# Top-32 attention and a cosine-gated feed-forward on one core: the 32 largest found by sixteen and sixteen instead of by pairs

## The chip, the cores and the metric

The kernel runs on one core of a Trainium2 chip. The metric is the device time of one execution in microseconds (us), lower is better. Five engines of the core work side by side, each with its own queue of instructions that it takes in order: TensorE (PE), VectorE (DVE), ScalarE (ACT), GpSimd (POOL) and SyncE (SP, which here only issues DMAs). [...]

## The reference

Eight batches of eight heads, 576 queries and 576 keys each, 64 wide, are attended to over the 32 largest scores of each query; the result, 4608 tokens of 512 values, goes through a feed-forward of 2048 hidden values with the gate h * cos(h).

```python
scores = scale * np.matmul(q, k.transpose(0, 1, 3, 2))          # (8, 8, 576, 576)
kth = np.partition(scores, -top_k, axis=-1)[..., -top_k:-top_k + 1]   # top_k = 32
scores = np.where(scores >= kth, scores, -1000000000.0)
attn = np.exp(scores - np.max(scores, axis=-1, keepdims=True))
attn = attn / (np.sum(attn, axis=-1, keepdims=True) + 1e-09)
x = np.matmul(attn, v)       # brought to (4608, 512)
h = x @ w_in                 # 512 -> 2048
out = (h * np.cos(h)) @ w_out
```

All data are 32-bit floats.

## The kernel before

The 4608 tokens are 36 blocks of 128 rows, and a block has four units, each a pair of heads: 144 units. One call of `slot(i, u, w, x, z)` is written out for each unit i, and the order of its statements is the order of each engine's queue; no scheduler reorders it. In a slot, unit u = i is searched for its 32 largest, unit w = i-1 is masked and exponentiated, unit x = i-2 is sent to be transposed, and z, the four units of a block, are multiplied with V in one slot of four. The feed-forward of an earlier block b is spread over the four slots of a block; m = i % 4 chooses which part. "Slot m2" below is a slot with m = 2.

**Scores.** PE makes the 576 scores of both heads into PSUM (L242, tile `sc`, and its last 128 columns in `rim`); ACT copies them to SBUF as `s` (`take_scores`, L253 and L257). Scores of two units are made in each of m0 and m2, into two buffers.

**Search.** DVE finds the eight largest of a row with one instruction (MAX8, L361) and overwrites them with a very small number with another (MATCH_REPLACE8, L366), so that the next MAX8 finds the next eight. A slot first folds its 576 scores to 288: `fold_high` (L267, DVE) keeps the larger of columns c and c + 288 in `rest`, and the smaller goes to `low`: POOL adds the two as integers (`fold_sum`, L283) and subtracts the larger (`fold_low`, L292). For the units 8 to 10 (`BUSY`) DVE does the smaller too (`fold_now`, L275). Of the larger ones 32 are found in four rounds, of the smaller ones 16 in two, each for both heads: 12 MAX8 and 8 MATCH_REPLACE8, all over 288. In the next slot `merge_first` and `merge_second` (L349, L354) find the 32nd of the two sorted lists, and `distances` (L372) the shift for the exponent.

**Weights of the attention.** ACT masks (`mask`, L380), and takes exponentials with their sums (`exponentials`, L389). DVE adds a small constant and takes the reciprocal (`sums`, `reciprocal`, L397 and L402) between the last two MAX8 of the slot, so that the reciprocals are the last that DVE does in a slot. In the next slot POOL splits the 32-bit exponentials into 16-bit halves (`split_scores`, L412) and then the reciprocals (`split_sums`, L418); SP writes them to memory (L446) and fetches them back transposed (L452) into a ring of five units. In m2 the values of a block are made (L480), and DVE multiplies them with the reciprocals into `xT` (L496), ahead of the last MAX8 pair.

**Feed-forward.** For each block PE makes the hidden values in four banks of 512 (`first_bank`, L543) and the output in four runs (`second_run`, L606). Between them, for each bank: ACT reads the bank twice (`take_first`, L557 and L559), POOL takes the cosine's argument in two instructions (`argument`, L572 and L575), ACT the sine of two banks at once (`sine`, L583), and POOL multiplies (`gate`, L592). Loading a table of exponentials or sines is an ACT instruction of its own.

**POOL's queue before**, from the split on: m0: split, argument of bank 0, fold_sum, fold_low, argument of bank 1. m1: split, gate 0, fold_sum, fold_low, gate 1, argument of bank 2. m2: split, argument of bank 3, fold_sum, fold_low, gates 2 and 3. m3: split, fold_sum, fold_low. In the first dozen slots POOL, DVE and ACT also decode the feed-forward's weights, which come as 64-bit words (`decode_first`, `decode_second`, `decode_third`).

## Time and profile before

| what | value |
|---|---|
| median of 3 runs | 1406.32 us (1405.22 to 1406.49) |
| profiled execution: its own time, and its span | 1406.25 us, 1404.1 us |
| busy: PE, DVE, POOL, ACT | 1347.3, 1337.5, 1197.8, 1140.7 us |
| the chain that ended last: DVE, ACT, PE, POOL | 68%, 18%, 8%, 3% |
| MAX8, all 1728 | 720.7 us busy |
| MATCH_REPLACE8, all 1152 | 502.0 us busy |
| first `fold_high`, 15th (unit 14), last (unit 143) | 7.78, 152.07, 1332.99 us |

The span is the time from the first to the last instruction of the profiled execution; its own time has 2.15 us more. The lines of a profile name the engine, the line of the kernel, the operation, the tile written and the tiles read, partitions x elements, and a count. A busy time counts each instruction to its end, while the next may start before that: the distance from start to start (the chain's pieces) says what an instruction costs its engine.

### The profile page before, as it was taken

How to read it: one execution, taken by the hardware profiler on the slowest of the kernel's cores; microseconds unless marked ns; L12 is line 12 of the kernel's file. 1: busy time of each engine (PE TensorE's matmuls, PEld its weight loads, DVE VectorE, ACT ScalarE, POOL GpSimd, SP SyncE). 2: the span in 40 equal slices, each digit the busy share in tenths (PEclk: the TensorE clock that was granted, in tenths of full speed). 3: DMA queues.
4: the chain of work that ended last, by engine and by line, in shares of the span. 5: the costliest groups of instructions: out<-in, count | busy, mean ns of one | idle time of the engine just before them, and what ended most of it. 6: DMA issues, size and time to landing. Idle time of an engine off the chain costs nothing.

```text
span 1404.1 us, 43874 instructions
## 1 busy us (share of the span) xinstructions
PE 1347.3 (96%) x17024; PEld 906.3 (65%) x17024; DVE 1337.5 (95%) x5012; ACT 1140.7 (81%) x2043; POOL 1197.8 (85%) x1008
## 2 busy tenths in 40 slices
PE   5569999999999999999999999999999999999998
PEld 3355666666666666666666666666666666776665
DVE  7998999999999999999999999999999999999941
ACT  6978888888888888888888888888888888888842
POOL 4787999999999999999999999999999999999920
PEclk9789999999999999999999999999999999999999
DMA  9567775768566586767756568666768566555640
GB/s 285 191 195 188 191 191 152 200 177 200 165 167 168 158 195 172 182 166 176 193 165 176 151 171 198 165 176 163 207 169 175 145 165 172 156 155 144 159 121 16
DMA packets 427488, 240.87 MB, mean 172 GB/s; under 512 B 375952, under 2 KB 392592, under 8 KB 427280
## 3 DMA queue, kind: packets, MB, share of 16 engines
q1 hardware_dynamic: 420720, 224.22, 61.2%
q10 hardware_dynamic: 6560, 13.85, 3.0%
q8 instruction: 133, 2.18, 0.7%
q14 instruction: 75, 0.61, 0.1%
HBM read 45.09 MB, written 101.19 MB: 104 GB/s over the span
## 4 chain that ended last, share of the span: by engine, by line
DVE 68%; ACT 18%; PE 8%; POOL 3%; issue 1%; DMA 1%; ACTq 0%; POOLq 0%; DVEq 0%
DVE top L361 32%; DVE rest L366 18%; DVE rest L267 7%; DVE low L366 6%; ACT s L389 4%; ACT s L380 4%; PE o L606 3%; ACT L583 3%; PE mm L543 3%; ACT x L583 2%; ACT s L253 2%; PE rim L480 2%; ACT s L257 2%; DVE xT L496 1%; DMA ring<-rows 1%
## 5 line engine op out<-in xcount | busy, mean ns | idle before, releaser
L543 PEld LDWEIGHTS mm<-xT,w_in 128*64 128x64 f32 x9216 | 509.5, 137 | 68.2 <-issue 30.3
L543 PE MATMUL mm<-xT,w_in 128*64 128x128 f32 x9216 | 523.7, 273 | 2.7 <-ACT x L559 1.7
L606 PE MATMUL o<-w_out,g 128*64 128x512 f32 x2304 | 521.8, 595 | 3.1 <-POOL g L592 3.1
L361 DVE MAX8 top<-rest 128x8 f32<-128x288 f32 x1152 | 478.9, 451 | 0.0
L366 DVE MATCH_REPLACE8 rest<-top,rest 128x288 f32<-128x288 f32 x864 | 376.6, 443 | 0.0
L380 ACT ACTIVATE s<-s,top 128x576 f32<-128x576 f32 x288 | 207.7, 769 | 189.0 <-DVE top L354 130.3
L606 PEld LDWEIGHTS o<-w_out,g 128*64 128x64 f32 x2304 | 160.6, 137 | 257.6 <-issue 253.2
L412 POOL COPY halves<-s 128x2304 uint16<-128x2304 uint16 x140 | 294.6, 2104 | 35.7 <-ACT s L389 22.3
L361 DVE MAX8 top<-low 128x8 f32<-128x288 f32 x576 | 241.8, 449 | 1.5 <-POOL low L292 1.5
L389 ACT ACTIVATE s<-s,nd 128x576 f32<-128x576 f32 x288 | 220.8, 769 | 2.2
L292 POOL TENSOR_TENSOR low<-low,rest 128x576 int32<-128x576 int32 x141 | 199.8, 1417 | 11.0
L283 POOL TENSOR_TENSOR low<-s 128x576 int32<-128x576 int32 x141 | 200.0, 1418 | 6.5 <-ACT s L259 6.5
L592 POOL TENSOR_TENSOR g<-g,x 128x512 f32<-128x512 f32 x136 | 172.5, 1279 | 16.4 <-ACT x L583 16.4
L575 POOL TENSOR_TENSOR x<-g,x 128x512 f32<-128x512 f32 x136 | 174.0, 1279 | 11.4
L242 PE MATMUL sc<-k,q 64*64 64x448 f32 (+1 forms) x1120 | 147.9, 568 | 14.4 <-DMA k<-in_k_dram 7.4
L480 PE MATMUL rim<-ring,v 128*64 128x128 f32 (+1 forms) x2560 | 138.8, 267 | 0.2 <-issue 0.2
L480 PEld LDWEIGHTS rim<-ring,v 128*64 128x64 f32 x2560 | 129.5, 139 | 6.8 <-issue 6.3
L253 ACT COPY s<-sc 128x896 f32<-128x896 f32 (+1 forms) x144 | 128.0, 889 | 3.4 <-PE sc L242 3.4
L366 DVE MATCH_REPLACE8 low<-top,low 128x288 f32<-128x288 f32 x288 | 125.4, 443 | 0.0
L267 DVE TENSOR_TENSOR rest<-sc,s 128x576 f32<-128x576 f32 x144 | 107.7, 748 | 6.8 <-ACT s L259 6.8
L257 ACT COPY s<-rim 64x256 f32<-64x256 f32 (+1 forms) x280 | 102.8, 367 | 6.9 <-PE rim L480 5.2
L242 PEld LDWEIGHTS rim<-k,q 64*64 64x64 f32 (+1 forms) x1120 | 49.0, 139 | 75.6 <-issue 60.1
(55 smaller groups left out, 1210.1 us busy)
## 6 DMA issues: line engine op xcount, KB each, us to landing
rows<-halves SPq DMA_DIRECT2D x140, 640.0 KB, 3.5
out_dram<-ob ACTq DMA_DIRECT2D x36, 256.0 KB, 3.9
q<-in_q_dram SPq DMA_DIRECT2D x31, 288.0 KB, 5.0
st<-in_moe_w_in_dram SPq DMA_DIRECT2D x16, 512.0 KB, 6.9
v<-in_v_dram SPq DMA_DIRECT2D x32, 256.0 KB, 4.4
k<-in_k_dram SPq DMA_DIRECT2D x31, 144.0 KB, 4.5
k<-in_k_dram SPq DMA_DIRECT2D x32, 128.0 KB, 4.4
st<-in_moe_w_out_dram SPq DMA_DIRECT2D x8, 512.0 KB, 5.6
```

What stands on the lines that cost most here:

```text
L242: nc.tensor.matmul(to[r0 : r0 + rows, rim_bank(r0, j) if k0 else place(u["hp"], j), 0 : k1 - k0], st["q"][d, q0 : q0 + rows], st["k"][d, k ...
L267: nc.vector.tensor_tensor(out=u["rest"][:, :, HS:S], in0=sc[:, :, 0:HS], in1=s[:, :, HS:S], op=ALU.max)
L283: nc.gpsimd.tensor_tensor(out=u["low"].bitcast(I32), in0=s[:, :, 0:HS], in1=s[:, :, HS:S], op=ALU.add)
L292: nc.gpsimd.tensor_tensor(out=low, in0=low, in1=u["rest"][:, :, HS:S].bitcast(I32), op=ALU.subtract)
L361: nc.vector.max(to[:, j], src[:, j])
L366: nc.vector.match_replace(rest[:, j], to[:, j], src[:, j], NEG)
L380: nc.scalar.activation(out=s[:, j], in_=s[:, j], func=AF.Prelu, bias=less[:, j], scale=1.0, alpha=FAR)
L389: nc.scalar.activation(out=s[:, j], in_=s[:, j], func=AF.Exp, bias=nd[:, j : j + 1], scale=SCALE, accum_out=den[:, j, 0:1],)
L412: nc.gpsimd.tensor_copy(out=halves[:, :, 0 : 2 * S], in_=s.rearrange("p (k h) -> p h k", h=2))
L480: nc.tensor.matmul(to[d, r], lhsT, rhs, start=(bank, j) not in begun, stop=c == NT - 1 and u in us[-2:] and r0 + rows == P,)
L543: nc.tensor.matmul(mm[r0 : r0 + D, a * P : (a + 1) * P], w_in[f // FC][:, c, (f % FC) * P + r0 : (f % FC) * P + r0 + D], blk["xT"][:, c], ...
L606: nc.tensor.matmul(blk["o"][r0 : r0 + D], g[:, at : at + D], w_out[f], start=f == 0, stop=f == NF - 1)
```

## The change

The 32 largest are found in another way: sixteen of the 288 larger ones, in two rounds over 288; then sixteen of all that is left, in two rounds over 576, the 272 larger ones left (with the sixteen overwritten) and the 288 smaller ones side by side in `rest`. The 16th largest of the larger ones has at most 15 smaller partners above it, so these are the same 32. The last one found is the 32nd: one small DVE instruction (`threshold`) takes the place of the two merges. The smaller ones are therefore read from the third of four rounds on. In slots m1 from unit 9 on, DVE makes them itself (`by_vector`).

The split is written at the end of the slot of the exponentials (unit w) and no longer at the start of the next one; POOL has the same instructions on either side of that border, so what changes is what stands behind the split. POOL's queue is now: m0: fold_sum, fold_low, argument 1, split. m1: gates 0 and 1, split, arguments 2 and 3. m2: fold_sum, fold_low, gates 2 and 3, split. m3: fold_sum, fold_low, split, argument 0. Against the queue before, fold_sum and fold_low of m1 are gone, and argument 2 and gate 1 have changed sides: gate 1 stands ahead of the split, argument 2 behind it.

On ACT the exponentials are moved ahead of `take_first` of bank 1 (m0) and bank 2 (m1), in m2 the sine of banks 2 and 3 ahead of the exponentials, and in m3 `take_first` of bank 0 ahead of the mask. PE's order is the same up to the last few groups; there the values of the last four units are made together. A load of V may no longer be issued with the send of a block's last unit, and one piece of the weights is loaded three slots earlier.

```diff
@@ -258,40 +258,40 @@
         if at:
             nc.scalar.copy(out=s[:, :, 0:at], in_=u["sc"][:, :, 0:at])
 
+    def by_vector(u):
+
+        return u["n"] in BUSY or u["n"] % NP == 1 and u["n"] > NP + 2
+
     def fold_high(u):
 
         s, sc = u["s"], u["sc"]
-        if u["n"] not in BUSY:
+        if not by_vector(u):
             del u["sc"]
-        u["rest"] = work.tile([P, 2, S], F32, tag="rest", name="rest", bufs=1)
+        u["high"] = work.tile([P, 2, HS], F32, tag="high", name="high", bufs=1)
         nc.vector.tensor_tensor(
-            out=u["rest"][:, :, HS:S], in0=sc[:, :, 0:HS], in1=s[:, :, HS:S], op=ALU.max
+            out=u["high"], in0=sc[:, :, 0:HS], in1=s[:, :, HS:S], op=ALU.max
         )
 
     def fold_now(u):
 
         s, sc = u["s"], u.pop("sc")
-        u["low"] = work.tile([P, 2, HS], F32, tag="low", name="low", bufs=1)
         nc.vector.tensor_tensor(
-            out=u["low"], in0=sc[:, :, 0:HS], in1=s[:, :, HS:S], op=ALU.min
+            out=u["rest"][:, :, HS:S], in0=sc[:, :, 0:HS], in1=s[:, :, HS:S], op=ALU.min
         )
 
     def fold_sum(u):
 
         s = u["s"].bitcast(I32)
-        u["low"] = work.tile([P, 2, HS], F32, tag="low", name="low", bufs=1)
         nc.gpsimd.tensor_tensor(
-            out=u["low"].bitcast(I32), in0=s[:, :, 0:HS], in1=s[:, :, HS:S], op=ALU.add
+            out=u["rest"].bitcast(I32)[:, :, HS:S], in0=s[:, :, 0:HS], in1=s[:, :, HS:S], op=ALU.add
         )
 
     def fold_low(u):
 
-        if u["n"] in BUSY:
+        if by_vector(u):
             return
-        low = u["low"].bitcast(I32)
-        nc.gpsimd.tensor_tensor(
-            out=low, in0=low, in1=u["rest"][:, :, HS:S].bitcast(I32), op=ALU.subtract
-        )
+        low = u["rest"].bitcast(I32)[:, :, HS:S]
+        nc.gpsimd.tensor_tensor(out=low, in0=low, in1=u["high"].bitcast(I32), op=ALU.subtract)
 
     dens = []
     for i in range(2):
@@ -301,58 +301,36 @@
 
     tops = []
     for i in range(2):
-        t = consts.tile([P, 2, TOPK + 1, 2], F32, tag=f"top{i}", name=f"top{i}")
-        nc.vector.memset(t[:, :, 0, 1], -NEG)
-        tops.append(t)
-
-
-
-    def topk_first(u, w, ahead=()):
+        tops.append(consts.tile([P, 2, TOPK + 1], F32, tag=f"top{i}", name=f"top{i}"))
+
+    def topk_first(u, w):
 
         u["top"] = tops[u["n"] % len(tops)]
+        u["rest"] = work.tile([P, 2, S], F32, tag="rest", name="rest", bufs=1)
         if w:
-            merge_first(w)
-        for step in ahead:
-            step()
-        if u["n"] not in BUSY:
+            threshold(w)
+        if not by_vector(u):
             fold_sum(u)
         fold_high(u)
-        if w:
-            merge_second(w)
-        if u["n"] in BUSY:
+        if by_vector(u):
             fold_now(u)
-        topk_round(u, 0, [lambda: distances(w), lambda: None] if w else ())
+        search(
+            u["top"][:, :, 1:9], u["high"], u["rest"][:, :, 0:HS], True,
+            [lambda: distances(w), lambda: None] if w else (),
+        )
 
     def topk_round(u, rnd, between=(), ahead=None):
-        top, rest, lasts = u["top"], u["rest"], TOPK // 8 - 1
-        end = TOPK - 1 - 8 * rnd
-        at = top[:, :, end : end - 8 if rnd < lasts else None : -1, 0]
-        search(
-            at, rest[:, :, HS:S] if rnd == 0 else rest[:, :, 0:HS], rest[:, :, 0:HS], rnd < lasts,
-            between if rnd < lasts else (),
-        )
-        if rnd < lasts:
-            return
-        del u["rest"]
-        low = u.pop("low")
-        for k in range(TOPK // 16):
-            more = k < TOPK // 16 - 1
-            if ahead and not more:
-                ahead()
-            search(top[:, :, 1 + 8 * k : 9 + 8 * k, 1], low, low, more, () if more else between)
-
-
-
-    def merge_first(u):
-        n = TOPK // 2 + 1
-        u["lesser"] = u["top"].rearrange("p j r i -> p j (r i)")[:, :, 2 * n : 3 * n]
+        if ahead:
+            ahead()
+        some = u["rest"][:, :, 0 : HS if rnd == 1 else S]
+        search(u["top"][:, :, 1 + 8 * rnd : 9 + 8 * rnd], some, some, rnd < TOPK // 8 - 1, between)
+        if rnd == TOPK // 8 - 1:
+            del u["rest"], u["high"]
+
+    def threshold(u):
+        u["less"] = u["top"][:, :, 0:1]
         nc.vector.tensor_reduce(
-            out=u["lesser"], in_=u["top"][:, :, 0:n], axis=mybir.AxisListType.X, op=ALU.min
-        )
-
-    def merge_second(u):
-        nc.vector.tensor_reduce(
-            out=u["top"][:, :, TOPK - 1, 1], in_=u.pop("lesser"), axis=mybir.AxisListType.X,
+            out=u["top"][:, :, 0], in_=u["top"][:, :, TOPK : TOPK + 1], axis=mybir.AxisListType.X,
             op=ALU.max, negate=True,
         )
 
@@ -366,11 +344,9 @@
                 nc.vector.match_replace(rest[:, j], to[:, j], src[:, j], NEG)
 
     def distances(u):
-        top = u.pop("top").rearrange("p j r i -> p j (r i)")
-        u["less"] = top[:, :, 2 * TOPK - 1 : 2 * TOPK]
         u["nd"] = small.tile([P, 2], F32, tag="nd", name="nd")
         nc.vector.tensor_reduce(
-            out=u["nd"], in_=top[:, :, 2 * TOPK - 2 : 2 * TOPK], axis=mybir.AxisListType.X, op=ALU.add
+            out=u["nd"], in_=u.pop("top")[:, :, 0:2], axis=mybir.AxisListType.X, op=ALU.add
         )
 
     def mask(u):
@@ -404,16 +380,13 @@
     def both(u):
         return [lambda: sums(u), lambda: reciprocal(u)] if u else ()
 
-    def split_scores(u):
+    def split(u):
 
 
         s = u.pop("s").rearrange("p j k -> p (j k)").bitcast(U16)
         halves = u["halves"] = work.tile([P, 2, 2 * S + P], U16, tag="halves", name="halves", bufs=1)
         nc.gpsimd.tensor_copy(out=halves[:, :, 0 : 2 * S], in_=s.rearrange("p (k h) -> p h k", h=2))
 
-    def split_sums(u):
-
-        halves = u["halves"]
         rden = u.pop("rden").bitcast(U16).rearrange("p (j h) -> p h j", h=2)
         nc.gpsimd.tensor_copy(
             out=halves[:, :, 2 * S :].rearrange("p h (j d) -> p h j d", j=2),
@@ -638,7 +611,7 @@
     at_slot, at_once = {}, {}
 
     def load_at(i, *what):
-        while i in at_slot or (what[0] is load_v and i % NP == 0):
+        while i in at_slot or (what[0] is load_v and i % NP == 3):
             i += 1
         at_slot[i] = what
 
@@ -662,72 +635,70 @@
     for i, u in enumerate(units):
         u["n"] = i
 
-    def send(x, between=()):
-
-        split_scores(x)
-        split_sums(x)
-        for step in between:
-            step()
+    def send(x):
+
+        split(x)
         write_halves(x)
-        for load, b, hp in at_send.pop(x["n"] + 2, ()):
+        for load, b, hp in at_send.pop(x["n"] + 1, ()):
             load(b, hp)
         transposes(x)
 
     def slot(i, u, w, x, z):
         m, b = i % NP, (i - NP - 2) // NP
-        n = (3, 4, 3, 4, 4, 3, 2, 2, 0, 2, 2, 0)[i] if i < 3 * NP else 0
+        n = (3, 4, 3, 4, 4, 3, 2, 3, 0, 2, 1)[i] if i < 2 * NP + 3 else 0 if m == 0 else 2
         if i < NP:
             for load, bb, hp in at_once[i]:
                 load(bb, hp)
         load_weights(n, nc.sync if i < NP + 2 else nc.scalar)
-        if x:
-            (turn if i < NP + 2 else send)(x)
-        if m == 1:
-            gate(b, 0)
-        elif m == 0:
-            argument(b, 0)
-        topk_first(u, w, [lambda: argument(b - 1, 3)] if m == 2 else ())
+        if x and i < NP + 2:
+            turn(x)
+        topk_first(u, w)
         fold_low(u)
-        topk_round(u, 1)
-        topk_round(u, 2)
         if i > 1:
             decode_second(NP)
             decode_third()
+        topk_round(u, 1)
+        topk_round(u, 2)
 
         for o in scored.get(i, []):
             scores(o)
         if z:
             values(z)
-        if m == 1:
+        if m == 0:
+            second_run(b - 1, 3)
+        elif m == 1:
+            gate(b, 0)
             gate(b, 1)
-        elif m == 0:
-            second_run(b - 1, 3)
+            first_bank(b, 3)
         elif m == 2:
             second_run(b - 1, 1)
-        elif m == 3:
+        else:
             second_run(b - 1, 2)
+            take_first(b, 0)
+            first_bank(b, 1)
 
         if w:
             mask(w)
+        if m == 2:
+            sine(b - 1, 1)
+            gate(b - 1, 2)
+            gate(b - 1, 3)
+        if w:
+            exponentials(w)
         if m == 0:
             take_first(b, 1)
             argument(b, 1)
             first_bank(b, 2)
         elif m == 1:
             take_first(b, 2)
-            argument(b, 2)
-            first_bank(b, 3)
             second_run(b, 0)
-        if w:
-            exponentials(w)
-        if m == 3:
-            take_first(b, 0)
-        elif m == 2:
-            sine(b - 1, 1)
-            gate(b - 1, 2)
-            gate(b - 1, 3)
         if i + 1 < NU:
             take_scores(units[i + 1])
+        if m == 0:
+            sine(b, 0)
+            take_second(b - 1)
+        elif m == 1:
+            take_first(b, 3)
 
         def ahead():
             if z:
@@ -740,28 +711,25 @@
         if i == 0:
             decode_second(NP)
             decode_third()
-        if m == 2:
+        if w and i > NP:
+            send(w)
+        if m == 1:
+            argument(b, 2)
+            argument(b, 3)
+        elif m == 2:
             first_bank(b, 0)
         elif m == 3:
-            first_bank(b, 1)
-        elif m == 0:
-            sine(b, 0)
-            take_second(b - 1)
-        elif m == 1:
-            take_first(b, 3)
+            argument(b, 0)
         decode_first(NP)
...
```

More of the change, by code (lines that the diff above doesn't have):

```diff
@@ L757, in drain @@
         ff["end"] = True
-        w, x, last_two = units[NU - 1], units[NU - 2], units[NU - 2 :]
-        send(x)
-        argument(b, 0)
+        w, last = units[NU - 1], units[NU - NP :]
+        threshold(w)
+        distances(w)
         second_run(b - 1, 3)
-        merge_first(w)
-        merge_second(w)
-        distances(w)
         mask(w)
@@ L776, in drain @@
         take_second(b - 1)
+        first_bank(b, 3)
         take_first(b, 2)
-        first_bank(b, 3)
         argument(b, 2)
@@ L782, in drain @@
         argument(b, 3)
-        second_run(b, 1)
         sine(b, 1)
@@ L786, in drain @@
         gate(b, 3)
-        values(units[NU - 4 : NU - 2])
-        take_values(units[NU - 4 : NU - 2])
-        second_run(b, 2)
-        values(last_two)
-        take_values(last_two)
-        second_run(b, 3)
+        values(last)
+        take_values(last)
+        second_run(b, 1)
         b += 1
         first_bank(b, 0)
-        take_second(b - 1)
         take_first(b, 0)
         argument(b, 0)
+        second_run(b - 1, 2)
+        first_bank(b, 1)
+        second_run(b - 1, 3)
+        take_second(b - 1)
         for k in range(1, BANKS):
-            first_bank(b, k)
             take_first(b, k)
             argument(b, k)
+            if k < BANKS - 1:
+                first_bank(b, k + 1)
             if k % 2 == 1:
```

## The prediction

> **What bounds the kernel now.** First the page's chain that ended last, by engine:

> ```profile
> DVE 68%; ACT 18%; PE 8%; POOL 3%; issue 1%; DMA 1%; ACTq 0%; POOLq 0%; DVEq 0%
> ```

> DVE carries it. The timeline of DVE shows how evenly (start, duration, what); these are `fold_high` of units 14, 78, 79, 82 and 143:

> ```profile
> 152.07 0.75 DVE L267 TENSOR_TENSOR rest<-sc,s 128x576 f32<-128x576 f32 x1
> ...
> 737.94 0.75 DVE L267 TENSOR_TENSOR rest<-sc,s 128x576 f32<-128x576 f32 x1
> 747.79 0.75 DVE L267 TENSOR_TENSOR rest<-sc,s 128x576 f32<-128x576 f32 x1
> ...
> 774.58 0.75 DVE L267 TENSOR_TENSOR rest<-sc,s 128x576 f32<-128x576 f32 x1
> ...
> 1332.99 0.75 DVE L267 TENSOR_TENSOR rest<-sc,s 128x576 f32<-128x576 f32 x1
> ```

> From unit 14 to 143 there are 129 slots in 1180.92 us, 32.25 periods of four slots at 36.62 us. Slot m2 (unit 78) takes 9.85 us, since it has the product with the reciprocals; the other three take (774.58 - 747.79) / 3 = 8.93. How close PE is behind shows on its timeline; these are the same two banks, one block apart, in the tightest period:

> ```profile
> 252.08 7.16 PE L543 MATMUL mm<-xT,w_in 128*64 128x128 f32 x128
> ...
> 288.22 7.16 PE L543 MATMUL mm<-xT,w_in 128*64 128x128 f32 x128
> ```

> 36.14 us: in that period PE's groups follow each other without a gap. So PE allows at most 0.48 us a period less than now, whatever DVE gains.

> What DVE's slot consists of is read from the chain in order of time (start, length up to the next piece, what), slot m0 of unit 80:

> ```profile
> 756.60 0.20 DVE top L349
> 756.80 0.66 DVE rest L267
> 757.46 0.10 DVE top L354
> 757.56 0.40 DVE top L361
> ...
> 759.23 0.72 DVE top L361 x2
> 759.95 0.86 DVE rest L366 x2
> 760.81 0.72 DVE top L361 x2
> ```

> A MAX8 over 288 costs DVE 0.36 us and a MATCH_REPLACE8 0.43. The third round begins 4.21 us after the slot. And POOL's queue at the same border of slots, from its timeline:

> ```profile
> 756.66 0.40 POOL L418 COPY halves<-rden 128x256 uint16<-128x256 uint16 x1 [1.30 <-DVE rden L402]
> 757.04 0.62 POOL L572 TENSOR_SCALAR x<-x 128x512 f32<-128x512 int32 x1
> 757.74 1.28 POOL L575 TENSOR_TENSOR x<-g,x 128x512 f32<-128x512 f32 x1
> 758.97 1.41 POOL L283 TENSOR_TENSOR low<-s 128x576 int32<-128x576 int32 x1
> 760.47 1.42 POOL L292 TENSOR_TENSOR low<-low,rest 128x576 int32<-128x576 int32 x1
> ```

> POOL waited here for the reciprocals, which DVE makes last in its slot, and went on 0.06 us after DVE's slot began. Copying them costs 0.38 us, an argument 1.93 (757.04 to 758.97), `fold_sum` 1.50, `fold_low` 1.42. The smaller halves are there at 761.89, 5.29 us into DVE's slot. The kernel before reads them behind four rounds and so doesn't wait: from the third round's 4.21 two more rounds of 0.72 and 0.86, less the last overwriting, put that at 4.21 + 1.58 + 0.72 = 6.51.

> **The search.** It removes 12 MAX8 and 8 MATCH_REPLACE8 over 288: 12 x 0.36 + 8 x 0.43 = 7.76 us. It adds four of each over 288 (3.16) and four MAX8 and two MATCH_REPLACE8 over 576, which the trace doesn't have. How DVE's time grows with length, from the groups by line (count | busy us, mean ns):

> ```profile
> L361 DVE MAX8 top<-rest 128x8 f32<-128x288 f32 x1152 | 478.9, 451 | 0.0
> L366 DVE MATCH_REPLACE8 rest<-top,rest 128x288 f32<-128x288 f32 x864 | 376.6, 443 | 0.0
> ...
> L504 DVE TENSOR_TENSOR xT<-rim,ring 128x128 f32<-128x128 f32 x28 | 6.8, 284 | 5.2 <-ACT s L257 4.7
> ...
> L592 DVE TENSOR_TENSOR g<-g,x 128x512 f32<-128x512 f32 x8 | 5.2, 688 | 4.9 <-ACT x L583 4.9
> ```

> Between 128 and 512 columns (688 - 284) / 384 = 1.05 ns a column; the search instructions at 288 lie on the same line (284 + 160 x 1.05 = 452 against 451 and 443). So 288 columns more are 0.30 us: a long MAX8 0.66, a long MATCH_REPLACE8 0.73, in all 4 x 0.66 + 2 x 0.73 = 4.10. Ends: the slope to the 576 of `fold_high` (0.75 - 0.688 over 64 columns, 0.94) gives 0.63 and 0.70; twice the short one gives 0.72 and 0.86. I take 0.30, the slope with the longest base. The search then costs 7.26 in place of 7.76: 0.50 us less a slot (0.68 to 0.00 at the ends).

> [...]

> **The merges.** L349 and L354 go, 0.20 and 0.10 us on the chain, and one reduction of two columns comes. MAX8 must still wait for the whole 0.75 of `fold_high`, against 0.66 + 0.10 now, so between 0 and 0.25 are left; I take 0.10, since the 0.20 alone lies outside that wait and half of it goes to the new reduction. A slot without a wait: 8.93 - 0.50 - 0.10 = 8.33.

> **Slots m1.** DVE makes the smaller halves: one more instruction of `fold_high`'s form, 0.66 on the chain (ends 0.66 and 0.75). POOL loses 1.50 + 1.42 there; POOL isn't what DVE waits for in m1, so that gives nothing directly.

> **The moved split and the earlier reading.** This decides. The third round now reads the smaller halves, 4.21 - 0.10 = 4.11 us into the slot. POOL can't begin them until the reciprocals are copied, since the split stands ahead in its queue, and that is 0.06 + 0.38 us into DVE's slot at the earliest. From there:
> - m3: split, then the two folds: 0.44 + 1.50 + 1.42 = 3.36. No wait.
> - m0: argument 0 stands between: 5.29. DVE waits 5.29 + 0.02 - 4.11 = 1.20 (0.02 from POOL's end to DVE's start is an estimate; ends 0 and 0.1).
> - m2: arguments 2 and 3 both stand between: 5.29 + 1.93 = 7.22. DVE waits 3.13.
> - m1: no fold on POOL.

> The wait isn't made good later, because the reciprocals that release POOL for the next slot come at the end of the delayed one. A period is 36.62 - 4 x 0.60 + 0.66 + 1.20 + 3.13 = 39.21 us, 2.59 more. PE's 36.14 lies under it. In 32.25 periods: +83.5 us.

> **ACT.** Its sequence in a slot m2, from the chain:

> ```profile
> 738.88 1.44 ACT s L380 x2
> 740.32 0.10 ACT nd L383
> 740.45 1.63 ACT s L389 x4
> 742.09 1.28 ACT L583
> 743.38 1.15 ACT x L583
> 744.53 0.79 ACT s L253
> ```

> In m2 the sine now stands ahead of the exponentials and waits for argument 3, which POOL ends 0.44 + 3.86 = 4.30 into the slot. Sine 1.15, the exponentials' table 1.28, exponentials 1.63 and the scores' copy (0.79, and its last columns, estimated at the same again) end at 9.9, in a slot that now lasts 8.33 + 0.92 + 3.13 = 12.4: hidden, by 2.5 us. In m3 reading bank 0 stands ahead of the mask. That bank needs `xT`, which DVE makes in m2 behind the third round, at 7.24 + 4.10 - 1.32 = 10.0 to 10.8; PE's bank takes half of 7.16, to 14.4, two us into m3. Two readings of 512 columns (estimated from 0.79 for 896: 1.1), mask, exponentials and copy (1.44 + 0.10 + 1.63 + 1.58) end at 20.2, and the next slot's fold comes at 12.4 + 8.33 = 20.7. Hidden by 0.5 us only; this is the second rival.

> **SP and DMA.** The send is the same 140 writes and transposed reads. Reading V moves from the border into m0 to other sends; the order on SP changes, no bytes. In steady slots I cost it nothing: the slots got longer, and the ring is written a slot and more ahead of its use. Cover gone, it would delay the values, which m2 has some 3 us of room for.

> **Start and end.** Up to unit 14 the slots are longer than 8.93 (152.07 us for 14) because of decoding. There the search's 0.60 us can be gained in slots 0 to 4 and 6 to 9, 9 x 0.60 = 5.4 at most, and none if ACT or POOL hold it; I take 4. Slots 8 to 10 have no fold on POOL in either kernel. At the end PE works off the last groups in both, with the same groups: 0, ends -3 and +3.

> **The sum.** Span 1404.1 + 83.5 - 4 = 1483.6; the profiled execution's time is 2.15 us more than its span, and 0.07 under the median: **1486 us**. One us per period more or less is 32 us.

> **The rivals.**
> 1. *PE becomes the bound, faster.* If the folds were ready within 4.11 us in each slot, DVE's period would be 34.9, and PE's 36.14 would decide: 1406.3 - 32.25 x 0.48 - 4 = 1387 us. For it POOL may have no more than 0.75 us between the reciprocals' copy and `fold_sum`; one argument has 1.93. Not slower at all needs both waits together under 1.7 us. The rows of POOL speak against it: it takes its queue in order, and the arguments stand in it. What speaks for it: POOL loses 2.92 us a period, and is idle before the reciprocals as quoted.
> 2. *A second wait on top.* The copy of the scores behind bank 0 in m3 arrives late. Its margin is 0.5 us with two estimates in it; each us beyond costs 32. At 1 us late: 1518 us.
> 3. *Only the wait in m2 holds*, because argument 0 finds its place while POOL waits: 1486 - 32.25 x 1.20 = 1447 us. Against it: argument 0 is behind the reciprocals, as in the quoted rows.
> 4. *Long searches don't overlap.* If each started only at the end of the one before, the four long MAX8 cost 0.09 more (0.451 - 0.36) and the two long MATCH_REPLACE8 about as much: 0.54 a slot, 2.2 a period, 1557 us. The 0.36 us from start to start in the quoted rows speaks against it. [...]

> **Chances.** Forecast 0.66 (its own range 1465 to 1505: waits and merges at their ends), rival 2 0.15, rival 3 0.08, rival 1 0.07, rival 4 0.04. The range reaches from rival 3 to a little above rival 2 and to two thirds of the upper end of the search (+64): 1440 to 1535. A change of 0.2% is about what a measurement here can tell from none. Slower 0.93, same 0.01, faster 0.06.

> **What would show it.** Right: DVE idle before the MAX8 of the third round, released by POOL's subtraction, some 3.1 us in m2 and 1.2 in m0, about 140 us in all, none in m3; PE with gaps of 3 us a period; MAX8 over 576 at 750 ns. Wrong: no DVE idle there, or the folds found ahead of the arguments on POOL; long searches far from 750 ns; DVE waiting for ACT's copy of the scores at the start of m0.

## The result, and the profile after

The changed kernel takes 1570.24 us (median of 4 runs, 1569.53 to 1571.31), the kernel before 1406.40 beside it: a ratio of 1.1168, 95% interval 1.1148 to 1.1187. Slower was right; 1486 us was 84 too low, and the time lies above the range, which ended at 1535.

The page after: its span, the chain that ended last by engine, the granted clock in 40 slices, and two of its costliest groups.

```profile
span 1568.7 us, 42579 instructions
...
PEclk6679999999999989999999989999999998999999
...
PE 76%; issue 7%; DVE 6%; POOL 4%; DMA 3%; ACT 2%; SPq 1%; DVEq 0%; POOLq 0%; ACTq 0%
...
L339 DVE MAX8 top<-rest 128x8 f32<-128x576 f32 (+1 forms) x864 | 534.0, 649 | 161.4 <-POOL rest L294 161.3
...
L271 DVE TENSOR_TENSOR high<-sc,s 128x576 f32<-128x576 f32 x144 | 108.7, 755 | 27.0 <-ACT s L257 20.8
```

DVE carried 68% of the chain before. Now PE carries 76%, although its instructions are the same. DVE idles 161 us for POOL's subtraction, against some 140 forecast, and 21 us for ACT's copy of the scores, which the prediction had named as the sign that it would be wrong.

DVE's timeline gives the slots, by the start of the folds of units 74 to 78 (m2, m3, m0, m1, next m2), the waits before the third round in m2 and m0, and the long MAX8:

```profile
779.61 0.76 DVE L271 TENSOR_TENSOR high<-sc,s 128x576 f32<-128x576 f32 x1
...
786.80 1.42 DVE L339 MAX8 top<-rest 128x8 f32<-128x576 f32 x2 [3.10 <-POOL rest L294]
...
790.97 0.76 DVE L339 MAX8 top<-rest 128x8 f32<-128x576 f32 x1
791.63 0.15 DVE L378 RECIPROCAL rden<-den 128x2 f32<-128x2 f32 x1
...
791.83 0.75 DVE L271 TENSOR_TENSOR high<-sc,s 128x576 f32<-128x576 f32 x1
...
801.02 0.76 DVE L271 TENSOR_TENSOR high<-sc,s 128x576 f32<-128x576 f32 x1 [0.41 <-ACT s L257]
...
806.91 1.42 DVE L339 MAX8 top<-rest 128x8 f32<-128x576 f32 x2 [1.79 <-POOL rest L294]
...
811.29 0.76 DVE L271 TENSOR_TENSOR high<-sc,s 128x576 f32<-128x576 f32 x1
...
820.20 0.76 DVE L271 TENSOR_TENSOR high<-sc,s 128x576 f32<-128x576 f32 x1
```

m2 takes 12.22 us, m3 9.19, m0 10.27, m1 8.91: 40.59 in all, where 39.21 was forecast. The wait in m2 is 3.10 (forecast 3.13) and m1 is 8.91 (8.99). What is over lies in m3, 0.83 us longer than the wait-free slot of 8.36 that five periods show, and in m0, where the wait is 1.79 in place of 1.20.

That makes 32.25 x (40.59 - 36.62) = 128 us; the folds of units 14 and 143 are 1343.04 us apart, 162.1 more than before. The other 34 us lie in four places. A batch is four and a half blocks, so that at every other change of batch a block holds rows of two batches: the units 16, 52, 88 and 124 on (below: the changes of batch; the three changes between two blocks cost nothing). There PE's timeline shows waits for keys, here in slots 52 and 54:

```profile
555.09 2.55 PE L242 MATMUL sc<-k,q 64*64 64x448 f32 x3 [3.57 <-DMA k<-in_k_dram]
...
577.41 1.22 PE L242 MATMUL sc<-k,q 64*64 64x448 f32 x3 [2.23 <-DMA k<-in_k_dram]
```

Slots 52 to 54 last 11.1, 12.3 and 17.1 us, against 10.3, 8.9 and 12.2 in other periods: 9.1 us more. By the same count the other three places (slots 16, 88 and 124 on) take 7.8, 7.6 and 9.0 more, 33.5 in all. The start is 1.7 us later, where the forecast had it 4 earlier, and what follows the last fold is 0.8 longer.

So two things were missing: some 45 us (128 less the forecast 83) spread over the slots m3 and m0, and some 34 at the changes of batch. The second has a plain suspect in the code. In both kernels a load of queries or keys is hung on the send of a numbered slot. `send` in slot i popped those of slot i at the start of that slot, and now pops them at its end.

The first shows on PE. Here is the same output run of 16 instructions in three periods that follow each other:

```profile
737.65 3.65 PE L579 MATMUL o<-w_out,g 128*64 128x512 f32 x16 [2.61 <-issue]
...
776.87 5.28 PE L579 MATMUL o<-w_out,g 128*64 128x512 f32 x16 [2.75 <-issue]
...
817.46 5.35 PE L579 MATMUL o<-w_out,g 128*64 128x512 f32 x16 [2.61 <-issue]
```

PE stands 2.6 us before this run in each, and the run of the same work then takes 3.65 us or 5.3. After 3.65 the next comes 39.22 us later, which is the forecast period (39.21); after 5.28 it is 40.59. The clock is the difference. In two stretches of 6 us that hold these runs (busy us and instructions of PE, PEld, DVE, ACT, POOL; granted clock; DMA share; GB/s):

```profile
736.00:742.00 6.00, 4.35 (x24) 1.62 (x28) 5.96 (x17) 5.64 (x12) 3.62 (x4) 1.00 0.56 136
...
816.00:822.00 6.00, 4.54 (x14) 1.79 (x16) 5.97 (x17) 5.63 (x13) 3.80 (x4) 0.72 0.64 149
```

Clock 1.00 and 0.72, and within the run of 5.35 us it is 0.50, as the last section shows. The gap is new, and the prediction gave it only as a sign ("PE with gaps of 3 us a period") without a price. On ACT's timeline of that slot m1 the reading of bank 2 (L530, L532) now stands behind the exponentials:

```profile
815.46 0.76 ACT L365 ACTIVATE s<-s,nd 128x576 f32<-128x576 f32 x1
...
816.22 0.57 ACT L530 ACTIVATE g<-mm 128x512 f32<-128x512 f32 x1
816.69 0.67 ACT L532 ACTIVATE x<-mm,quarter 128x512 int32<-128x512 f32 x1
```

It ends at 817.36, and PE goes on at 817.46. What a halved clock does to the bank that the next slot needs is on PE's timeline too, bank 0 in the period after the run of 3.65 and after that of 5.28:

```profile
750.75 3.77 PE L516 MATMUL mm<-xT,w_in 128*64 128x128 f32 x64
...
791.59 3.66 PE L516 MATMUL mm<-xT,w_in 128*64 128x128 f32 x64
```

It ends 14.1 us after the fold of its slot m2 in the first (754.52 - 740.39) and 15.6 in the second (795.25 - 779.61). ACT begins to read it at 795.30, and mask, exponentials and the scores' copy of m3 stand behind that. POOL's next split waits for the exponentials, and argument 0 and the folds of m0 stand behind the split:

```profile
795.30 0.60 ACT L530 ACTIVATE g<-mm 128x512 f32<-128x512 f32 x1 [5.83 <-PE mm L516]
...
799.62 2.10 POOL L388 COPY halves<-s 128x2304 uint16<-128x2304 uint16 x1 [4.51 <-ACT s L365]
```

The five slots m3 of 8.36 us between units 14 and 143 are just those that follow a run of 3.65 us behind such a gap (the sixth such run stands ahead of the last slot).

### The profile page after: what moved, and what is told of

The parts are those of the page before. It is cut to its first block, busy times and chain, and to the rows that moved or that the text cites. A ratio compares the mean times of both kernels' runs of the same rounds, so it can differ in the third digit from the quotient of the medians.

```text
span 1568.7 us, 42579 instructions
## 1 busy us (share of the span) xinstructions
PE 1411.1 (90%) x17024; PEld 927.9 (59%) x17024; DVE 1283.0 (82%) x3746; ACT 1145.1 (73%) x2043; POOL 1113.2 (71%) x944
## 4 chain that ended last, share of the span: by engine, by line
PE 76%; issue 7%; DVE 6%; POOL 4%; DMA 3%; ACT 2%; SPq 1%; DVEq 0%; POOLq 0%; ACTq 0%
PE o L579 31%; PE mm L516 27%; PE rim L453 9%; PE sc L242 7%; DVE top L339 3%; PE rim L242 2%; DMA k<-in_k_dram 2%; DVE rest L344 2%; POOL halves L388 1%; DMA rows<-halves 1%; ACT s L365 1%; ACT s L356 1%; DVE high L271 0%; POOL x L548 0%; POOL rest L294 0%
## 5 line engine op out<-in xcount | busy, mean ns | idle before, releaser
L339 DVE MAX8 top<-rest 128x8 f32<-128x576 f32 (+1 forms) x864 | 534.0, 649 | 161.4 <-POOL rest L294 161.3
L579 PE MATMUL o<-w_out,g 128*64 128x512 f32 x2304 | 570.3, 641 | 85.1 <-issue 85.1
L344 DVE MATCH_REPLACE8 rest<-top,rest 128x288 f32<-128x288 f32 (+1 forms) x576 | 337.0, 593 | 0.0
L530 ACT ACTIVATE g<-mm 128x512 f32<-128x512 f32 x144 | 85.2, 592 | 214.1 <-PE mm L516 211.6
L356 ACT ACTIVATE s<-s,top 128x576 f32<-128x576 f32 x288 | 207.6, 770 | 39.7 <-DVE top L332 37.2
L242 PE MATMUL sc<-k,q 64*64 64x448 f32 (+1 forms) x1120 | 166.8, 572 | 36.1 <-DMA k<-in_k_dram 25.5
L548 POOL TENSOR_TENSOR x<-g,x 128x512 f32<-128x512 f32 x137 | 175.0, 1277 | 11.4
L285 POOL TENSOR_TENSOR rest<-s 128x576 int32<-128x576 int32 x108 | 153.9, 1425 | 8.6 <-ACT s L259 5.9
L294 POOL TENSOR_TENSOR rest<-rest,high 128x576 int32<-128x576 int32 x108 | 153.4, 1420 | 8.5
L257 ACT COPY s<-rim 64x256 f32<-64x256 f32 (+1 forms) x280 | 102.9, 367 | 40.9 <-PE rim L453 19.9
L271 DVE TENSOR_TENSOR high<-sc,s 128x576 f32<-128x576 f32 x144 | 108.7, 755 | 27.0 <-ACT s L257 20.8
L253 ACT COPY s<-sc 128x896 f32<-128x896 f32 (+1 forms) x144 | 128.0, 889 | 2.9 <-PE sc L242 2.9
L339 DVE MAX8 top<-high 128x8 f32<-128x288 f32 x288 | 127.1, 455 | 3.7
L556 ACT ACTIVATE x<-x,halfpi 128x1024 f32<-128x1024 f32 x72 | 82.7, 1149 | 64.1 <-POOL x L548 61.4
```

Source lines behind the costliest of these rows:

```text
L242: nc.tensor.matmul(to[r0 : r0 + rows, rim_bank(r0, j) if k0 else place(u["hp"], j), 0 : k1 - k0], st["q"][d, q0 : q0 + rows], st["k"][d, k ...
L285: nc.gpsimd.tensor_tensor(out=u["rest"].bitcast(I32)[:, :, HS:S], in0=s[:, :, 0:HS], in1=s[:, :, HS:S], op=ALU.add)
L339: nc.vector.max(to[:, j], src[:, j])
L344: nc.vector.match_replace(rest[:, j], to[:, j], src[:, j], NEG)
L356: nc.scalar.activation(out=s[:, j], in_=s[:, j], func=AF.Prelu, bias=less[:, j], scale=1.0, alpha=FAR)
L548: nc.gpsimd.tensor_tensor(out=x, in0=g, in1=x, op=ALU.subtract)
```

## The experiments

First theory: late loads cost some 35 us, and the gap, through the clock and bank 0, some 40 to 45. Rival: the waits in m0 and m3 come from the queues of POOL and ACT alone, whatever PE does. A time that is given below without a ratio is that of one execution.

**Loads back to the earlier send (e1_loads).** Changed kernel, with:

```diff
-        while i in at_slot or (what[0] is load_v and i % NP == 3):
+        while i in at_slot or (what[0] is load_v and i % NP == 0):
...
-        at_send.setdefault(i + 1, []).append(what)
+        at_send.setdefault(i, []).append(what)
```

> The changed kernel with the loads of q, k and v issued one send earlier, which is the place they had before. Theory (late loads are a part of the loss, at four places where the batch changes, about 34 us in all beside 32 equal periods): PE no longer waits for k, about 1536 us. Rival (PE waits for k only because everything is late): within 5 us of 1570.

1533.17 us: 37 less. (The condition on V's loads keeps them off the send of a block's last unit; it has to change with the send, and holds in the kernel before as well.) The slots at a change of batch are now as long as the others, and the period between them is unchanged. The late loads cost 37 us.

**Bank 2 read ahead of the exponentials again (e4_read2).**

```diff
+        if m == 1:
+            take_first(b, 2)
         if w:
             exponentials(w)
...
         elif m == 1:
-            take_first(b, 2)
             second_run(b, 0)
```

> The changed kernel with ACT's reading of bank 2 put back ahead of the exponentials in m1. Theory (PE's gap comes from the output's buffer, which this reading frees behind the exponentials): the gap of 2.61 us goes, the clock stays, period 39.2, about 1530 us. Rival (the gap comes from the gate on POOL or another wait): gap and time stay, 1570.

1545.71 us. Away from the changes of batch the gap and the runs of over 5 us behind it are gone (mean granted clock of the run 0.963, in the changed kernel 0.942), and the period is 39.2 in the median (m3 8.36, m0 9.65 in about half of the periods and up to 10.3 in the others). The same output run now stands without a gap:

```profile
721.42 3.60 PE L579 MATMUL o<-w_out,g 128*64 128x512 f32 x16
```

The changes of batch got longer, slots of 18 to 19 us, which takes back part. The gap is what makes m3 long; this edit isn't the cure.

**Bank 0 read behind the exponentials (e5_read0).** The clock keeps falling (mean granted clock 0.954), but the mask and the scores' copy of m3 no longer stand behind bank 0:

```diff
-            take_first(b, 0)
-            first_bank(b, 1)
...
+        elif m == 3:
+            take_first(b, 0)
+            first_bank(b, 1)
```

> The changed kernel with ACT's reading of bank 0 put back behind the exponentials in m3. Theory (a late bank 0 holds up mask, exponentials and copy, and through them DVE): m3 falls from 9.2 to 8.35 us and m0 from 10.27 to 9.6, period 39.2, about 1530 us, with the lowered clock still there. Rival (PE itself is the bound by then): 1570.

1525.33 us: 45 less, 2 of it up to unit 14. m3 8.36, m0 9.65, m1 8.91, m2 12.2, although behind eleven gaps of 2.15 to 2.75 us the output run still takes over 5 us. One of them, in m1, and the folds of the four slots that follow it (m2, m3, m0, m1):

```profile
713.81 5.35 PE L579 MATMUL o<-w_out,g 128*64 128x512 f32 x16 [2.32 <-issue]
...
716.55 0.76 DVE L271 TENSOR_TENSOR high<-sc,s 128x576 f32<-128x576 f32 x1
728.85 0.75 DVE L271 TENSOR_TENSOR high<-sc,s 128x576 f32<-128x576 f32 x1
737.21 0.75 DVE L271 TENSOR_TENSOR high<-sc,s 128x576 f32<-128x576 f32 x1
746.87 0.76 DVE L271 TENSOR_TENSOR high<-sc,s 128x576 f32<-128x576 f32 x1
```

So the lost time goes by way of ACT's queue, as the prediction's second rival has it; the clock only makes bank 0 late.

**PE kept busy in the gap (e3_dummies, e3b_dummies18).** 36 and 18 products whose result is thrown away ahead of bank 3 in m1; nothing is left out.

```diff
+        if k == 3 and not ff["end"]:
+            for _ in range(36):          # 18 in the second
+                nc.tensor.matmul(
+                    mm[0:D, 0:P], w_in[3][:, 0, 0:D], blk["xT"][:, 0], start=True, stop=True
+                )
```

> The changed kernel with 36 matmuls whose result is thrown away ahead of bank 3 in each slot m1, some 2.0 us of work for PE, so that its gap of 2.61 us before the first run of the output shrinks to about 0.6 us. Theory (the gap lowers PE's clock and that makes bank 0 late for ACT): the run after the gap takes 3.6 us and not 5.35, the period falls from 40.66 to 39.2, about 1530 us, although PE does more. Rival (the clock has no part, PE is simply short of time): 1570 us or up to 65 us more.

1681.93 us, a miss. Each is executed as two matmuls of 0.109 us, so that 36 of them are 72 on PE and take 7.9 us (864.24 to 872.10 in one slot): three times the gap. The expectation of the next run has this as 3.9 us, which is half of it. Bank 3 came late, its argument too, and with it the folds behind it on POOL; m2 grew to 15.2 us. The mean granted clock was 0.974, against 0.942 in the changed kernel.

> As the run with dummies, with half of them: each such instruction was two for PE, so 36 were 3.9 us and filled more than the gap; 18 are 2.0 us and leave 0.6 of 2.6. Theory (a gap of 2.6 us lowers PE's clock, one of 0.6 doesn't): the run after it takes 3.6 us, periods of 39.2 in place of 40.66, about 1530 us. Rival (each added PE time ahead of bank 3 delays arguments and folds): 1600 us or more.

1558.84 us. The gap is gone and the run takes about 3.6 us (mean granted clock 0.972), but the 18 products take 3.9 us and not the 2.0 expected, some 1.3 more than PE's wait was: the period is 40.07, 0.5 less than in the changed kernel. m0 stays at 10.27. Filling the gap costs most of what it saves, so that the run is no test of the size.

**Both repairs (e6_loads_read0),** the edits of e1_loads and e5_read0 together.

> The changed kernel with the loads as early as before and ACT's reading of bank 0 behind the exponentials. Theory (these two are what the sum left out; the rest are the two waits for the folds): their savings add, 1570 - 37 - 45 = 1488 us, periods of 39.2. Rival (they overlap at the change of batch): 1500 us or more.

1503.25 us. From unit 14 to 143 the folds now take 1265.97 us, 39.26 a period, and the slots are m3 8.36, m0 9.65, m1 8.91, m2 12.2 to 12.3. DVE's waits of this run, by engine, line and what it waited for (us in total, times, longest):

```profile
DVE top L339 <- POOL rest L294: 144.4, 67, 3.1
```

That is the forecast: 39.21, and about 140 us of waiting. Of the 15 us over the expectation, 12 are in the start: slots 8 to 10 take 44.7 us, in e1_loads 32.6. ACT waits 6.4 us there for a piece of the weights to land, which e1_loads doesn't show, and POOL 9.8 us for its own write (2.6 in e1_loads). What delayed these transfers, and whether another execution would show it, is open.

**The parts alone.** The new search in the old order (e8_search_only: `by_vector`, `threshold` and the new rounds, `slot` and `send` as before), and the new order with the old search (e10_order_only):

> The kernel before with the new search alone (smaller halves on DVE in m1 too), its order of POOL, ACT and SP as before. Theory (one argument stands between reciprocals and folds in m0 and m2, so DVE waits 1.2 us in each): period 36.62 - 2.4 + 0.66 + 2.4 = 37.3, about 1424 us. Rival (the search itself is what costs): 1480 us or more; rival (the search pays by itself): under 1400.

1443.88 us, 20 over the expectation. The period is 37.2, against the 37.3 expected: in the old order only argument 0 in m0 and argument 3 in m2 stand ahead of the folds, and DVE waits 1.19 us in both. The start lost a further 18 us (unit 14 at 169.64), with DVE's waits for the folds in slots 3 to 7 nearly the same as in e9_vector_even below, where their cause is tested.

> The changed kernel's order and loads with the search of the kernel before (smaller halves searched by themselves, on POOL in all units but 8 to 10). Theory: the smaller halves are needed 6.50 us into the slot; two arguments ahead of the folds in m2 bring them at 7.24, a wait of 0.74 a period (24 us), none in m0, and the late loads cost their 34 to 37: about 1465 us. Rival (the order costs nothing by itself): 1406 to 1445.

1541.27 us: the time lies outside all expectations. With the old search DVE waits for the folds only 0.74 us in m2, as worked out (23.8 us in all), but m2 takes 11.5 to 12.2 us and m3 mostly 10.1. DVE's timeline in m2, then PE's output run:

```profile
772.57 0.82 DVE L361 MAX8 top<-low 128x8 f32<-128x288 f32 x2 [0.74 <-POOL low L292]
...
775.26 0.76 DVE L493 TENSOR_TENSOR xT<-rim,ring 128x256 f32<-128x256 f32 x2 [1.02 <-ACT s L257]
```

```profile
763.46 3.65 PE L603 MATMUL o<-w_out,g 128*64 128x512 f32 x16 [2.06 <-POOL g L589]
```

DVE waits for ACT's copy, which now stands behind the sine and the exponentials, 49.8 us in all ahead of `xT`, and 27.3 ahead of the fold, where reading bank 0 stands ahead of the mask as in the changed kernel. PE waits for gate 0, which POOL makes behind the folds in m1; the changed kernel has no fold on POOL there. So the new order with the old search costs 135 us (some 35 of it again at the changes of batch), the new search alone 38, and together they cost 164. That the waits of the search lie partly in the slack of the new order would fit these numbers, but no run took its waits out one by one, and the two losses of the order that e1_loads and e5_read0 undo are in this run as well. The parts can't be priced alone and added.

**Less ahead of the folds (e11_arg2):** e6_loads_read0 with argument 2 made before the split of m1 and not after it.

```diff
+        if m == 1:
+            argument(b, 2)
         if w and i > NP:
             send(w)
         if m == 1:
-            argument(b, 2)
             argument(b, 3)
```

> The changed kernel with early loads and bank 0 read late (e6), and argument 2 moved ahead of the split in m1, so that one argument and not two stands ahead of the folds in m2. Theory: DVE's wait in m2 falls by 1.93 us to 1.2, period 37.25, 1503 - 62 = 1441 us. Rival (the split waits for the argument and moves the loss to the transposes): 1490 or more.

1473.72 us, 30 less than e6_loads_read0, half of what was expected; from unit 14 to 143 it is 21.7 less, and the rest is the start, which isn't late here. m2 takes 11.4 to 11.9; DVE waits some 2.4 us there and not 1.2, because argument 2 waits for ACT's late reading of bank 2 and now holds up the split.

**The folds away from POOL in the slots with arguments.** e8_search_only with DVE making the smaller halves in m0 and m2 in place of m1, and gate 0 behind the folds of m1 (e9_vector_even):

```diff
-        return u["n"] in BUSY or u["n"] % NP == 1 and u["n"] > NP + 2
+        return u["n"] in BUSY or u["n"] % 2 == 0 and u["n"] > NP + 2
...
-        if m == 1:
-            gate(b, 0)
-        elif m == 0:
+        if m == 0:
             argument(b, 0)
...
         if m == 1:
+            gate(b, 0)
             gate(b, 1)
```

> The kernel before with the new search, but with the smaller halves made by DVE in m0 and m2, the slots with an argument in POOL's queue ahead of the folds, and gate 0 behind the folds in m1. Theory (with no wait for the folds DVE's period is 36.62 - 2.4 + 1.3 = 35.5, under PE's 36.14, so PE decides): about 1390 us, 1385 to 1400. Rival (another wait takes its place, or POOL still is late): 1406 or more.

1407.86 us, ratio 1.0014 (1.0005 to 1.0024). PE bounds the steady part now: its page's chain has

```profile
PE 88%; ACT 2%; DVE 2%; DMA 1%; POOL 1%; issue 0%; ACTq 0%
```

From unit 14 to 143 it takes 1168.74 us against 1180.92 before, but unit 14 comes 12.4 us later. DVE's waits show why:

```profile
DVE top L341 <- POOL rest L294: 17.8, 7, 4.3
```

All seven are in the start, where POOL also adds up the decoded weights. So e12_even_decode puts the decoding (`decode_second` on DVE, `decode_third` on POOL) ahead of the second round, as the changed kernel has it:

```diff
-        topk_round(u, 1)
-        topk_round(u, 2)
         if i > 1:
             decode_second(NP)
             decode_third()
+        topk_round(u, 1)
+        topk_round(u, 2)
```

> The variant with DVE's smaller halves in m0 and m2 in the order before, with DVE's step of the weights' decoding ahead of the second round, as in the changed kernel. Theory: its period is PE's 36.14 already, and it lost 12 us up to unit 14 to folds that stood behind the decoding on POOL (seven waits of DVE, 17.8 us); with the decoding earlier some 10 of them go: about 1397 us. Rival (the start is held by DMA and PE): 1408.

**1389.12 us, ratio 0.9872 (0.9858 to 0.9886): 1.3% under the kernel before.** Unit 14 comes at 151.37, 13.1 us earlier than in e9_vector_even, so it was the folds behind the decoding that made the start late; the expectation had some 10 us for it. The period is PE's own. The same two banks one block apart, on PE's timeline:

```profile
720.93 7.16 PE L521 MATMUL mm<-xT,w_in 128*64 128x128 f32 x128
...
757.07 7.16 PE L521 MATMUL mm<-xT,w_in 128*64 128x128 f32 x128
```

36.14 us, the floor that the prediction read from the kernel before.

> As the variant above, with units 6 and 7 on DVE as well, where decoding and splits share POOL. Theory: up to 3 us more, about 1394 us. Rival (DVE itself is what those slots wait for): 1398 or more.

With units 6 and 7 on DVE as well (`range(6, 11)` in place of `BUSY`), 1393.70 us, ratio 0.9915 (0.9901 to 0.9929): 4.6 us more than e12_even_decode. The expectation's 1394 is met by luck, since it was a gain reckoned from 1397. The profiled executions are 2.1 us apart, and the two added instructions of DVE aren't the reason: slots 5 to 8 are 0.7 us shorter in sum, and slot 10 is 3.0 us longer, where DVE waits 7.3 us for ACT's copy of the scores and not 4.3. Why is open. DVE had waited for no fold of units 6 and 7, so little was to be gained.

## Why the prediction was right and wrong

Right, by its own steps:
- *The search and the merges.* A long MAX8 lasts 0.75 and a slot without a wait 8.36, where 8.33 was worked out; m1 is 8.91 against 8.99. Taking the slope with the longest base, and the distance from start to start in place of the duration, held. The fourth rival (long searches that don't overlap) is out: the reciprocals begin 0.66 us after the MAX8 ahead of them (790.97 and 791.63), which lasts 0.76.
- *POOL's queue.* The waits of 3.13 and 1.20 were measured as 3.10 here and, with ACT's lateness taken out, 144.4 us in all in e6_loads_read0. The period of 39.21 was there too: 39.26. The 0.02 from POOL's end to DVE's start was an estimate that no row of the kernel before shows; in the changed kernel it is 0.03 in m2 (786.77 to 786.80) and in m0 (806.88 to 806.91). The third rival, that only m2's wait holds, is out.
- *PE's 36.14 as a floor.* e12_even_decode stands on it. The first rival, 1387 us with the folds ready in time, was right as a condition: e12_even_decode meets it, the changed kernel doesn't.

Wrong:
- *"SP and DMA … In steady slots I cost it nothing."* The four changes of batch are the place. The step priced the values and the ring, and left out the queries and keys that go out with the same send. They leave a slot later; PE waits for the keys. 37 us by e1_loads. A list of every load that is hung on the moved send would have shown them.
- *ACT in m3, "Hidden by 0.5 us only".* The reckoning of that margin was good. Bank 0 was forecast to end 14.4 us into m2, and where PE's clock is kept it ends about there, at 14.1. With the clock halved it ends at 15.6, the margin is overdrawn, and both m3 and, by the split behind the late exponentials, m0 get longer: 45 us by e5_read0. This is the second rival, to which 0.15 was given, at 1.4 us a period (45 / 32.25). What failed is the step ahead of it: reading bank 2 was moved behind the exponentials in m1, and what that does to PE (a gap of 2.6 us) was not costed, because PE had slack in the period.
- *The start.* It was taken as 4 us less and is 1.7 more.
- *The range.* Its upper end took in each surprise by itself. Both came, and the 84 us are nearly their sum, 37 + 45. In e6_loads_read0, without the two, the period is the forecast one, so the sum was right in its steady part.

## What to carry to other kernels

For each instruction that is moved, list what hangs on it in its queue and in the code, the loads that go out with a send above all, and ask of each load which instruction then waits, in the places where the pattern breaks as well as in the steady slots: here that was 37 us (e1_loads). An engine with slack in its period, here PE with a floor of 36.14 under a period of 39.26 (e6_loads_read0), can still cost time when a new gap stands ahead of work that another engine's queue waits for in order: 45 us (e5_read0). Where an operand is read earlier, let the engine that needs it make it in just those slots in which the other's queue is full: with the old order, and the decoding behind the folds, that brought 1389 us, where the new search alone took 1444.

## What the hardware showed that was not expected

Behind a gap of 2.6 us PE's output run mostly had a granted clock of 0.50 for 3.2 to 3.4 us of it, and sometimes 1.00 throughout. In the changed kernel, from 140 us on, 29 output runs follow a gap of 2.59 to 2.75 us; 23 took 5.23 to 5.35 us and 6 took 3.65. In e6_loads_read0 14 runs behind gaps of 0.82 to 1.46 us all took 3.65, as did one behind 1.89; of 18 behind 2.20 to 2.78, 15 took 5.04 to 5.35. Two rows of that run, the shorter and the longer kind:

```profile
709.54 3.65 PE L579 MATMUL o<-w_out,g 128*64 128x512 f32 x16 [1.04 <-issue]
...
905.37 5.35 PE L579 MATMUL o<-w_out,g 128*64 128x512 f32 x16 [2.32 <-issue]
```

```profile
735.82:739.22 3.40, 1.57 (x8) 0.74 (x10) 3.40 (x8) 3.36 (x8) 2.10 (x1) 1.00 0.24 51
739.23:742.63 3.40, 3.40 (x31) 1.25 (x31) 3.37 (x13) 3.06 (x6) 2.15 (x3) 1.00 0.93 262
773.37:776.77 3.40, 0.75 (x14) 0.51 (x10) 3.40 (x11) 3.39 (x8) 1.15 (x2) 1.00 0.38 79
776.78:780.18 3.40, 3.31 (x8) 1.11 (x10) 3.40 (x9) 3.05 (x6) 1.72 (x3) 0.50 0.62 139
814.33:817.73 3.40, 0.79 (x12) 0.51 (x10) 3.40 (x11) 3.39 (x8) 1.30 (x1) 1.00 0.15 36
817.74:821.14 3.40, 3.40 (x10) 1.21 (x8) 3.37 (x10) 3.04 (x7) 1.72 (x3) 0.50 0.81 162
```

The gaps are alike, but the first (735.04 to 737.65) is cut by a border at 735.81, so that no stretch has more than 1.84 us of it. The same count, from these records in the traces, over the 152 gaps of 0.7 to 3.0 us ahead of such runs, from 140 us on, in the changed kernel, e1_loads, e5_read0, e6_loads_read0 and e10_order_only sorts them all: the 96 with at least 2.06 us inside one stretch were followed by a run of 5.04 to 5.35 us, the 56 with at most 2.03 us by one of 3.65. Among the 96 is a gap of no more than 2.06 us, in e10_order_only (723.34, a run of 5.35); behind one of 2.65 in e5_read0 that a border cuts the run took 3.65.
